# Attention output transposed by DMA, values and w_out cast by GpSimd's DMAs, first keys first

## The chip, the core and the metric

The kernel runs on one core of a Trainium2 chip. The core has TensorE (matmuls, results in PSUM), VectorE, ScalarE and GpSimd (elementwise work), and SyncE (SP), which here only issues transfers. Each engine runs its own stream of instructions in order and waits on semaphores. Sixteen DMA engines move the data; a transfer is issued by SP, ScalarE (the ACT queue) or GpSimd (the POOL queue). The metric is the device time of one execution in microseconds, lower is better.

## The reference

Two layers follow each other. The first is causal attention with 8 batches, 8 heads, 576 positions and a head size of 64; 16 "beacon" keys and values stand ahead of the sequence and are seen by every query. The second is a feed-forward layer on the 4608 x 512 result, with 2048 hidden units and an ELU between its two products.

```python
k_all = np.concatenate([beacon_k, k], axis=2)          # (8, 8, 592, 64)
v_all = np.concatenate([beacon_v, v], axis=2)
scores = scale * np.matmul(q, k_all.transpose(0, 1, 3, 2))
causal[:, Nb:] = np.triu(np.ones((S, S), dtype=bool), k=1)
scores = np.where(causal, -1000000000.0, scores)
a = softmax(scores)
attn = np.matmul(a, v_all)                             # (8, 8, 576, 64)
x = attn.transpose(0, 2, 1, 3).reshape(4608, 512)
h = x @ w_in                                           # 512 x 2048
g = np.where(h > 0.0, h, np.exp(np.minimum(h, 0.0)) - 1.0)
out = g @ w_out                                        # 2048 x 512
```

All inputs and the output are float32 in HBM.

## The kernel before, in words

**Attention.** Two heads are worked on at a time: pair n = 4 b + hp is pair hp of batch b, 32 pairs in all. SP loads its keys and queries in float32 (`load_pair`, L266; the first queries go by the ACT queue). A cast to bf16 (L271, GpSimd or VectorE) is followed by nine transposes on TensorE and one for the beacon keys (L308, L310), and by copies out of PSUM (kT on VectorE, L318 and L319; qT on ScalarE or VectorE, L324 and L326). Then come the scores (L335), their exponentials on ScalarE (L344), the causal mask on GpSimd (L350) and the product with the values (`do_AV`, L369), whose 65th column is the sum of the exponentials. VectorE divides (`do_norm`, L384 and L385) and writes fp16 rows of the attention output into `x16s`. The queries of a batch are cut into five blocks (`BLOCKS`) of 112, 128, 128, 128 and 80 rows.

**Values.** `load_v` (L277, L281) brings a chunk of 128 keys for all heads to a float32 staging tile by SP; `cast_v` (L285) casts it on VectorE into one of two fp16 buffers, which take turns between the batches.

**Turning x.** The feed-forward layer wants x with its 512 features on the partitions. `do_xT` (L395) transposes each block of a pair on TensorE, five transposes per pair, and `do_xcopy` (L402) copies the result from PSUM to `xT` on VectorE. In batch 0 this is done range by range, in the others once per pair.

**Feed-forward.** The tokens are cut into ten tiles (`TILES`): two of 256, eight of 512. For a tile, 16 (or 8) steps of four matmuls or more with w_in (L418) each fill a PSUM buffer. ScalarE takes the exponential (`do_e`, L424), GpSimd clamps it (`do_clamp`, L428), and VectorE joins it with h (`do_join`, L437) into fp16. Then 16 matmuls with w_out per 128 tokens (L445), a copy (L451) and a store by SP (L455). The weights are loaded by SP in pieces of 128 x 512 (`load_w`, L294) and cast by VectorE or GpSimd (`cast_w`, L299). The PSUM buffers of L418, L445, of the values' product and of the x transposes come from the same four ("ff").

**The order.** Nothing of the order is left to a scheduler on the chip. `Plan` is a small list scheduler that runs at build time: every piece of work is an `Op` with an engine, a key, a guessed duration, its dependencies and the buffers that it takes and gives. An engine that is free takes the ready operation with the lowest key; the instructions of each engine are then issued in the order that comes out. Loads go in the order of `FIRST` (i = piece of w_in, o = piece of w_out, k and q = pair, b = beacon keys, v = chunk of values), and after it by keys; SP issues the loads in exactly that order. The constants `SHIFT`, `AT`, `AT0`, `PACES` and `LAG` place batches and tiles in time, `ON_POOL` and `Q_ON_ACT` choose engines. The durations and places are numbers in the code, and what happens on the chip can differ from them.

Of the kernel before, what the change touches and what calls it, by code (L numbers as in the profile page):

```python
# [15 lines left out]
P = 128  # L16
# [96 lines left out]
def kernel(  # L113
# [103 lines left out]
    xT = [big.tile([P, NT], FP16, name=f"xT{cc}") for cc in range(NCC)]  # L217
# [11 lines left out]
    with tc.tile_pool(name="psum", bufs=1, space=bass.MemoryType.PSUM) as psum:  # L229
        slots = {  # L230
# [42 lines left out]

        def load_v(b, jc):
            vst = vsts[b, jc] = stage.tile([P, H, D], FP32, tag="vst", name="vst", bufs=5)
            if jc == 0:
                nc.sync.dma_start(out=vst[0:NB], in_=beacon_v[b].rearrange("h n d -> n h d"))  # L277
            r0 = NB if jc == 0 else 0
            lo = P * jc - NB + r0
            n = kc_sz[jc] - r0  # L280
            nc.sync.dma_start(out=vst[r0:r0 + n], in_=v[b, :, lo:lo + n, :].rearrange("h s d -> s h d"))  # L281
# [13 lines left out]

        def cast_w(which, i):
            fo, cc = divmod(i, NCC)
            dst = w_in16[:, cc, 512 * fo:512 * fo + 512] if which == 0 else w_out16[:, i, :]
            (nc.gpsimd if ON_POOL[which][i] == "1" else nc.vector).tensor_copy(out=dst, in_=wsts[which, i])  # L299

# [152 lines left out]
        def do_store(tt, t4):  # L453
# [5 lines left out]
        SHIFT = [16.14, -0.99, 5.34, 5.22, 2.06, -2.4, 5.6, 10.12]  # L459
        AT = [6.32, -0.92, -1.25, -0.44, -0.32, 1.85, 2.37]  # L460
        AT0 = [[-34.73, -23.83, -34.35, -35.48], [-34.06, -25.35, -36.58, -41.97], [-23.78, -23.81, -5.98, -9.75]]
        PACES = [(-11.97, 2.68, 26.27, 2.47), (-3.71, 3.3, 35.33, 4.82), (35.86, 1.78, 23.69, 3.57), (76.2, 2.29, 30.35, 3.0), (117.45, 1.81, 27.55, 2.07)]
        ON_POOL = ("0100001100101101", "0110011111111010", "00011011")
        LAG = 27.37
        URGE = 44.17
        Q_ON_ACT = "11011010"
        FIRST = (
            "i3 q0 k0 b0 q1 k2 k3 v0 k1 q2 q3 i8 v1 i10 v2 i7 i15 i0 v3 i1 i4 i9 i11 b1 i2 i14 v4 o2 k4 "
            "i6 q4 i13 i5 k5 o4 o8 i12 v5 o7 v6 o6 o1 o5 q5 q6 v8 o0 o12 k6 o13 o9 o15 o3 o10 o14 v9 "
            "o11 v7 k7 q7 ").split()  # L470
# [6 lines left out]
        scaled, last_xT = {}, {}  # L477
# [3 lines left out]
        def load_key(name, key):  # L481
            return FIRST.index(name) - 200 if name in FIRST else key
# [3 lines left out]
        def plan_loads(n):  # L486
            b, hp = divmod(n, HP)
            if hp == 0:
                got = load(load_key(f"b{b}", place(b, 0) - 31), 0.2, partial(load_bk, b), take=["bk"])
                bk_in[b] = add("POOL", place(b, -0.9), 0.6, partial(cast_bk, b),  # L490
                               deps=[got, last_T.get(b - 2)], give=["bk"])
            gots = []
            for is_k in (True, False):
                key = load_key(("k" if is_k else "q") + str(n), place(b, hp) - 30)
                gots.append(load(key, 0.85, partial(load_pair, n, is_k), take=["st"] if is_k else [], issue=0.61))
            on_dve = n < len(ON_POOL[2]) and ON_POOL[2][n] == "0"
            qk_in[n] = add(
                "DVE" if on_dve else "POOL", place(b, hp + AT[0]), 0.9 if on_dve else 1.23,
                partial(cast_pair, n, nc.vector if on_dve else nc.gpsimd), deps=gots + [last_T.get(("pair", n - 2))], take=["sb"], give=["st"])
# [3 lines left out]
        def plan_v(b):  # L503
            for jc in range(NKC):
                key = load_key(f"v{NKC * b + jc}", place(b - 1, 1.8 + 0.4 * jc))
                got = load(key, 1.5, partial(load_v, b, jc), take=["vst"], issue=1.0 if jc == 0 else 0.5)
                v_cast[b, jc] = add(
                    "DVE", place(b, -0.7 + 0.16 * jc), 0.56, partial(cast_v, b, jc),
                    deps=[got, last_AV.get(b - 2)], give=["vst"])

        def plan_w(which, i, key):
            got = load(load_key("io"[which] + str(i), 0), 0.75, partial(load_w, which, i), take=["gt"])
            eng, dur = ("POOL", 0.65) if ON_POOL[which][i] == "1" else ("DVE", 0.55)
            w_at[which, i] = add(eng, key, dur, partial(cast_w, which, i), deps=[got], give=["gt"])

        def plan_pair(n):
# [6 lines left out]
            last_T[b] = last_T["pair", n] = T  # L523
# [27 lines left out]
            for r, groups in enumerate([(0,), (1,), (2,)] if b == 0 else [(0,), (1, 2)]):  # L551
# [7 lines left out]
                last_AV[b] = AV  # L559
                normed.append(add(  # L560
                    "DVE", key - URGE, 0.32 + 0.148 * len(blks), partial(do_norm, n, groups),
                    deps=[AV, last_xT.get(n - 2 * HP)], give=["ff", "av"]))
# [16 lines left out]
        def plan_tile(p):  # L579
# [3 lines left out]
            for b in range(B):  # L583
                for r, (rlo, rhi) in enumerate(CUT.ranges):
                    if b * S + rlo < hi and b * S + rhi > lo:
                        xs += [scaled[b * HP + hp, r] for hp in range(HP)]
# [40 lines left out]
        for i in range(16):  # L627
            plan_w(0, i, place(0, 2.0) + i)
            plan_w(1, i, place(1, 0.5) + i)
# [7 lines left out]
        issues.sort(key=lambda i: i.key)  # L637
        for one, two in zip(issues, issues[1:]):
# [30 lines left out]
```

## Time and profile before

| | us |
|---|---|
| three runs: median | 370.35 |
| lowest | 370.12 |
| the profiled execution | 371.33 |
| its span, first to last instruction | 369.6 |
| TensorE busy | 350.4 (95%) |
| VectorE busy | 235.6 (64%) |
| ScalarE busy | 197.7 (53%) |
| GpSimd busy | 199.0 (54%) |
| first transpose / first scores on TensorE at | 7.9 / 10.9 |
| first L418 matmul / first L445 matmul at | 33.3 / 54.0 |
| last x transpose / last matmul at | 294.9 / 365.7 |

One more run took 1993.31 us and is not used. The page gives the busy time of each engine, the span in 40 slices of 9.24 us, the DMA queues, the chain of work that ended last, and groups of instructions by line with their counts and mean durations. Instructions that only issue a transfer do not count as busy. A matmul's recorded time overlaps with the next one's: four matmuls of 512 columns are 379 ns each by their row, and hold the chain for 0.86 us together. The chain of work says at each moment which instruction the end was waiting for, so the time that a group holds on it is what the group costs.

### The profile page before, as it was taken

How to read it: one execution, taken by the hardware profiler on the slowest of the kernel's cores; microseconds unless marked ns; L12 is line 12 of the kernel's file. 1: busy time of each engine (PE TensorE's matmuls, PEld its weight loads, DVE VectorE, ACT ScalarE, POOL GpSimd, SP SyncE). 2: the span in 40 equal slices, each digit the busy share in tenths (PEclk: the TensorE clock that was granted, in tenths of full speed). 3: DMA queues.
4: the chain of work that ended last, by engine and by line, in shares of the span. 5: the costliest groups of instructions: out<-in, count | busy, mean ns of one | idle time of the engine just before them, and what ended most of it. 6: DMA issues, size and time to landing. Idle time of an engine off the chain costs nothing.

```text
span 369.6 us, 8541 instructions
## 1 busy us (share of the span) xinstructions
PE 350.4 (95%) x3360; PEld 197.8 (54%) x3360; DVE 235.6 (64%) x496; ACT 197.7 (53%) x293; POOL 199.0 (54%) x376
## 2 busy tenths in 40 slices
PE   1688999999999999999999999999999999999995
PEld 1457865645565565555565455555555544444442
DVE  1758898777767668585974756566655555555421
ACT  1566876486658777567646556456563333333200
POOL 4467999576737766566743456454343334333200
PEclk9999999999999999999999999999999999999999
DMA  7999999995493276861455310000000001000022
GB/s 215 290 283 310 309 304 238 292 241 155 124 244 114 66 175 164 215 184 36 125 149 140 102 50 2 30 28 30 31 30 28 31 28 57 31 28 28 30 85 85
DMA packets 58856, 47.21 MB, mean 128 GB/s; under 512 B 41920, under 2 KB 41920, under 8 KB 58816
## 3 DMA queue, kind: packets, MB, share of 16 engines
q1 hardware_dynamic: 58672, 46.38, 44.2%
q8 instruction: 26, 0.43, 0.5%
q10 hardware_dynamic: 144, 0.29, 0.3%
q14 instruction: 14, 0.11, 0.1%
HBM read 37.22 MB, written 9.44 MB: 126 GB/s over the span
## 4 chain that ended last, share of the span: by engine, by line
PE 86%; DVE 4%; POOL 3%; DMA 3%; ACT 1%; issue 1%; SPq 0%; ACTq 0%; POOLq 0%
PE ops L445 34%; PE hps L418 30%; PE av L369 8%; PE sc L335 7%; PE tr L308 4%; DMA st<-in_k_dram 3%; PE xt L395 2%; POOL e L428 1%; DVE gt L437 1%; POOL et L350 1%; DVE kT L318 1%; DVE w_out L299 1%; ACT et L344 1%; ACT qT L324 1%; PE tr L310 0%
## 5 line engine op out<-in xcount | busy, mean ns | idle before, releaser
L418 PE MATMUL hps<-xT,w_in 128*128 128x512 f16 (+1 forms) x640 | 143.7, 358 | 0.5 <-DVE gt L437 0.4
L445 PE MATMUL ops<-w_out,gt 128*128 128x512 f16 x576 | 143.9, 379 | 0.1
L428 POOL TENSOR_SCALAR e<-e 128x512 f32<-128x512 f32 x144 | 89.3, 623 | 97.4 <-ACT e L424 97.4
L437 DVE SCALAR_TENSOR_TENSOR gt<-e,hps 128x512 f16<-128x512 f32 x144 | 97.5, 683 | 63.3 <-POOL e L428 63.1
L424 ACT ACTIVATE e<-hps 128x512 f32<-128x512 f32 x144 | 85.8, 601 | 95.0 <-PE hps L418 93.8
L344 ACT ACTIVATE et<-sc 128x736 f16<-128x736 f32 (+3 forms) x128 | 103.9, 864 | 29.1 <-PE sc L335 25.6
L418 PEld LDWEIGHTS <-w_in 128*128 128x128 f16 x640 | 58.8, 98 | 54.7 <-issue 3.6
L445 PEld LDWEIGHTS <-gt 128*128 128x128 f16 x576 | 52.5, 98 | 57.0 <-issue 2.1
L350 POOL TENSOR_SCALAR_AFFINE_SELECT et<-et 128x256 f16<-128x256 f16 (+2 forms) x160 | 59.9, 400 | 38.3 <-ACT et L344 35.4
L369 PEld LDWEIGHTS <-et 128*128 128x128 f16 (+1 forms) x960 | 37.0, 99 | 9.7 <-issue 1.5
L369 PE MATMUL av<-v,et 128*128 128x65 f16 (+1 forms) x960 | 41.4, 197 | 0.0
L335 PE MATMUL sc<-qT,kT 64*128 64x80 bf16 (+3 forms) x704 | 37.2, 237 | 3.5 <-ACT qT L324 2.0
L451 DVE COPY osb<-ops 128x512 f32<-128x512 f32 x36 | 24.8, 688 | 21.0 <-PE ops L445 20.7
L271 POOL CAST st<-st 128x1152 bf16<-128x1152 f32 x28 | 32.1, 1149 | 7.0 <-POOL et L350 2.2
L335 PEld LDWEIGHTS <-kT 64*128 64x128 bf16 x704 | 21.9, 97 | 22.6 <-issue 14.1
L385 DVE TENSOR_TENSOR x<-av,rl 128x384 f16<-128x384 f32 (+2 forms) x68 | 32.0, 471 | 2.3
L308 PE MATMUL tr<-identb,st 128*128 128x128 bf16 x288 | 23.1, 230 | 9.1 <-DVE st L271 8.5
L318 DVE COPY kT<-tr 128x576 bf16<-128x576 bf16 x32 | 24.1, 753 | 8.1 <-PE tr L310 7.3
L308 PEld LDWEIGHTS <-st 128*128 128x128 bf16 x288 | 19.8, 103 | 14.7 <-DVE st L271 8.9
L384 DVE RECIPROCAL rl<-av 128x6 f32<-128x6 f32 (+2 forms) x68 | 12.5, 183 | 21.5 <-PE av L369 20.9
L324 ACT ACTIVATE qT<-tr 128x576 bf16<-128x576 bf16 x20 | 13.0, 649 | 23.9 <-DVE kT L319 20.7
L285 DVE CAST v<-vst 128x512 f16<-128x512 f32 (+1 forms) x40 | 19.8, 504 | 1.7 <-DMA vst<-in_v_dram 1.7
(26 smaller groups left out, 101.0 us busy)
## 6 DMA issues: line engine op xcount, KB each, us to landing
st<-in_k_dram SPq DMA_DIRECT2D x32, 288.0 KB, 4.4
out_dram<-osb SPq DMA_DIRECT2D x36, 256.0 KB, 2.0
st<-in_q_dram SPq DMA_DIRECT2D x31, 288.0 KB, 4.7
vst<-in_v_dram SPq DMA_DIRECT2D x24, 256.0 KB, 5.4
wst<-in_moe_w_in_dram SPq DMA_DIRECT2D x16, 256.0 KB, 6.5
wst<-in_moe_w_out_dram SPq DMA_DIRECT2D x16, 256.0 KB, 6.0
vst<-in_v_dram SPq DMA_DIRECT2D x8, 224.0 KB, 5.0
vst<-in_v_dram SPq DMA_DIRECT2D x8, 160.0 KB, 5.6
```

What stands on the lines that cost most here:

```text
L271: eng.tensor_copy(out=o.rearrange("p g h d -> p h g d"), in_=f32s[n].rearrange("p h (g d) -> p h g d", g=G))
L308: nc.tensor.transpose(out=tr[:, P * g:P * g + P], in_=b16s[n][:, g].rearrange("p h d -> p (h d)"), identity=identb)
L335: nc.tensor.matmul(out=sc[:, h, o:o + w], lhsT=kT[D * h:D * h + D, P * jc:P * jc + P], rhs=qT[D * h:D * h + D, q0:q0 + w], start=True, sto ...
L344: nc.scalar.activation(out=et[:, :, 0:w], in_=scs[n, u][:, :, 0:w], func=AFT.Exp, bias=0.0, scale=float(1.0 / (D ** 0.5)))
L350: nc.gpsimd.affine_select(out=et[:, :, c0:c0 + dw], in_=et[:, :, c0:c0 + dw], compare_op=ALU.is_ge, fill=fill0, base=q0 + NB - P * jc, pat ...
L369: nc.tensor.matmul(out=av[:, c:c + D + 1], lhsT=ets[n, CUT.unit_of[jc, at]][0:m, h, col:col + P], rhs=v16[0:m, jc, 2 * hp + h, 0:D + 1], s ...
L385: nc.vector.tensor_tensor(out=x16s[b % 2][:, blks[0]:blks[0] + nb, P * hp:P * hp + P].rearrange("q i (h d) -> q i h d", d=D), in0=av[:, :, ...
L418: nc.tensor.matmul(out=hps[:, (hi - lo) * j:(hi - lo) * (j + 1)], lhsT=w_in16[:, cc, P * fc:P * fc + P], rhs=xT[cc][:, lo:hi], start=(cc = ...
L424: nc.scalar.activation(out=e, in_=hpss[tt, i], func=AFT.Exp, bias=0.0, scale=1.0)
L428: nc.gpsimd.tensor_scalar(out=e, in0=e, scalar1=1.0, scalar2=0.0, op0=ALU.min, op1=ALU.max)
L437: nc.vector.scalar_tensor_tensor(out=gt, in0=es[tt, i], scalar=1.0, in1=hpss[tt, i], op0=ALU.subtract, op1=ALU.max)
L445: nc.tensor.matmul(out=ops, lhsT=gts[tt, fc][:, P * t4:P * (t4 + 1)], rhs=w_out16[:, fc, :], start=(fc == 0), stop=(fc == NFC - 1))
```

## The change

Six things are changed together.

1. From batch 1 on (`XB = 1`) x is turned by DMA. The four `xT` tiles become one, and `turn_x` issues on SP one transposing DMA for each block of a batch, with all four pairs at once, after the last pair's division. TensorE's transposes and VectorE's copies stay for batch 0 alone.
2. From batch 2 on (`VB = 2`) the values are loaded by GpSimd's DMAs, which cast to fp16 on the way, straight into the fp16 buffer. The staging tile and VectorE's cast go.
3. All of w_out is loaded by four DMAs of GpSimd, which cast to fp16 on the way; its 16 loads by SP and its 16 casts go. These four wait for nothing.
4. Keys and queries of pair 0 are the first loads on SP and ACT, and w_out is gone from `FIRST`, which has another order.
5. Four pieces of w_in are cast by ScalarE ("2" in `ON_POOL`); fewer by GpSimd.
6. The constants that place the work are other numbers, and a batch's buffers now wait for all its products, not for the last alone.

```diff
-    xT = [big.tile([P, NT], FP16, name=f"xT{cc}") for cc in range(NCC)]
+    xTa = big.tile([P, NCC, NT], FP16, name="xT")
+    xT = [xTa[:, cc] for cc in range(NCC)]
...
+        VB = 2
+        XB = 1
...
+        def turn_x(b, blk):
+            q0, rows, _ = BLOCKS[blk]
+            nc.sync.dma_start_transpose(
+                out=xTa[:, :, b * S + q0:b * S + q0 + rows], in_=x16s[b % 2][0:rows, blk, :])
+
         def load_v(b, jc):
-            vst = vsts[b, jc] = stage.tile([P, H, D], FP32, tag="vst", name="vst", bufs=5)
+            if b >= VB:
+                eng, vst = nc.gpsimd, v16s[b % 2][:, jc, :, 0:D]
+            else:
+                eng = nc.sync
+                vst = vsts[b, jc] = stage.tile([P, H, D], FP32, tag="vst", name="vst", bufs=5)
...
+        def load_wo(f4):
+            nc.gpsimd.dma_start(
+                out=w_out16[:, 4 * f4:4 * f4 + 4, :], in_=moe_w_out[512 * f4:512 * f4 + 512, :].rearrange("(c p) d -> p c d", p=P))
...
+            if ON_POOL[which][i] == "2":
+                nc.scalar.activation(out=dst, in_=wsts[which, i], func=AFT.Copy)
...
-        SHIFT = [16.14, -0.99, 5.34, 5.22, 2.06, -2.4, 5.6, 10.12]
-        AT = [6.32, -0.92, -1.25, -0.44, -0.32, 1.85, 2.37]
+        SHIFT = [10.33, -2.61, 5.48, 3.9, 12.34, 1.61, 18.16, 26.55]
+        AT = [8.06, -1.0, -0.44, -0.82, -0.25, 0.89, 17.62, -15.16, 3.38, -53.58]
...
-        ON_POOL = ("0100001100101101", "0110011111111010", "00011011")
-        LAG = 27.37
+        ON_POOL = ("0200210020102110", "0021220022120010", "10001001")
+        LAG = 23.52
...
-            "i3 q0 k0 b0 q1 k2 k3 v0 k1 q2 q3 i8 v1 i10 v2 i7 i15 i0 v3 i1 i4 i9 i11 b1 i2 i14 v4 o2 k4 "
-            "i6 q4 i13 i5 k5 o4 o8 i12 v5 o7 v6 o6 o1 o5 q5 q6 v8 o0 o12 k6 o13 o9 o15 o3 o10 o14 v9 "
-            "o11 v7 k7 q7 ").split()
+            "b0 k3 q2 k2 i3 k1 q1 v1 q0 i11 k0 i7 q3 i8 i10 i15 v0 i13 i5 v3 i6 v2 i14 i9 i2 q4 b1 i1 "
+            "i12 v4 i0 k4 v5 k5 i4 q5 k6 q6 k7 v8 q7 v6 v9 v7 ").split()
...
-            return FIRST.index(name) - 200 if name in FIRST else key
+            return ["k0", "q0"].index(name) - 900 if name in ("k0", "q0") else FIRST.index(name) - 200 if name in FIRST else key
...
+                if b >= VB:
+                    key = place(b - 1, AT[8] + 0.4 * jc)
+                    got = add("POOL", key, 2.4 if jc == 0 else 1.2, partial(load_v, b, jc), deps=last_AV.get(b - 2, []))
+                    v_cast[b, jc] = add("DMA", key, 1.0, None, deps=[got], lat=2.5)
+                    continue
...
+                if b >= XB:
...
+                    if hp == HP - 1:
+                        for blk in blks:
+                            s = add("SP", at(AT[7]), 1.25, partial(turn_x, b, blk), deps=part.pop(blk))
+                            done = add("DMA", at(AT[7]), 0.5, None, deps=[s], lat=2.2)
...
+                    continue
...
-            plan_w(1, i, place(1, 0.5) + i)
+        for f4 in range(4):
+            got = add("POOL", AT[9] + 3 * f4, 1.5, partial(load_wo, f4))
+            got = add("DMA", -150 + f4, 3.0, None, deps=[got], lat=2.5)
+            w_at.update({(1, 4 * f4 + c): got for c in range(4)})
```

## The prediction

> **What bounds the kernel now.** I read the page's engine totals and slices first, then the table by stage, then the chain of work stage by stage, because a share of the whole span mixes a start that waits with a middle that does not.
>
> ```profile
> PE 350.4 (95%) x3360; PEld 197.8 (54%) x3360; DVE 235.6 (64%) x496; ACT 197.7 (53%) x293; POOL 199.0 (54%) x376
> DMA  7999999995493276861455310000000001000022
> GB/s 215 290 283 310 309 304 238 292 241 155 124 244 114 66 175 164 215 184 36 125 149 140 102 50 2 30 28 30 31 30 28 31 28 57 31 28 28 30 85 85
> ```
>
> TensorE is busy for 95% of the span, and the transfers are full (nine tenths and more) for the first ten slices of 9.24 us. The table by stage separates the two:
>
> ```profile
> core 0: us, PE busy (x) PEld busy (x) DVE busy (x) ACT busy (x) POOL busy (x), PEclk, DMA share, GB/s
> 0.00:10.00 10.00, 1.25 (x10) 0.98 (x10) 2.33 (x10) 1.28 (x1) 3.76 (x19) 1.00 0.77 217
> ...
> 30.00:40.00 10.00, 9.18 (x145) 7.80 (x144) 9.09 (x28) 6.82 (x11) 9.22 (x16) 1.00 1.02 286
> 40.00:60.00 20.00, 19.02 (x225) 13.97 (x224) 18.15 (x35) 15.16 (x25) 19.84 (x35) 1.00 1.03 295
> 60.00:100.00 40.00, 40.00 (x463) 23.22 (x462) 32.03 (x71) 25.49 (x39) 28.33 (x53) 1.00 0.80 215
> ...
> 340.00:370.00 30.00, 25.68 (x119) 11.43 (x117) 8.28 (x13) 2.80 (x5) 3.06 (x5) 1.00 0.17 62
> ```
>
> From 60 us to the last matmul at 365.7 TensorE has no idle time: there only fewer matmuls make the end earlier, and an idle VectorE or GpSimd gains nothing. All that an order of loads can win or lose lies in the first 60 us, where TensorE is idle for 15.3 us, 13.5 of them before 30 us. What follows the last matmul, 3.9 us of copy and store, is not touched.
>
> **Part 1, the transposes.** 140 of the 160 TensorE transposes on L395 go (28 pairs of heads in batches 1 to 7, five each), with 28 VectorE copies on L402. The row of the groups gives 221 ns each, but matmuls overlap, so I price them by the chain, which counts how far each moved the end:
>
> ```profile
> by line: PE hps L418 35.3%; PE ops L445 29.4%; PE av L369 12.3%; PE sc L335 11.7%; PE tr L308 7.5%; PE xt L395 3.5%; PE tr L310 0.8%
> 61 pieces in order of time: start us, us, what
> ...
> 62.00 0.26 PE xt L395 x5
> ```
>
> That is the stage 60 to 100 us. In the six stages of 40 us from 60 to 300 the transposes hold 3.5, 4.4, 3.2, 2.6, 2.6 and 2.6%, together 18.9% of 40 us = 7.6 us, and the table of that tile's instructions counts 25 + 30 + 25 + 20 + 20 + 20 = 140 of them there. Term: **-7.6 us**.
>
> In their place SP issues 35 transposing DMAs (five blocks for each of seven batches), each for all four pairs of a batch. The trace of before has none. By its rows an SP issue takes 0.61 us (a key load) and up to 2.6 where the ring is full, and lands after 2.0 us (a store) to 4.4 us (a key load). The plan writes 1.25 us to issue and 2.7 to land. So the last of five lands some 3 + 2 = 5 to 6.3 + 4.4 = 11 us after the last division. Before, that step took 3.9 us: the last division ended at 291.5 and the last copy of xT at 295.4. Tiles 8 and 9 both need batch 7; they are 2 x 32 groups of four matmuls at 0.864 us = 55.3 us, and from the first matmul of tile 8, at 295.6, there are 70.1 us to the end. So 14.8 us of other matmuls can be done while transposes are under way. At 11 us they cost nothing; I take 0, and price the excess as a rival. SP is also the queue of the loads and stores: a transpose that waits for a division holds them up, but the loads are keyed about 30 us ahead, and 35 x 1.25 = 44 us of SP's time lies in 369.
>
> **Part 2, values by GpSimd.** 30 casts of v (24 x 0.517 + 6 x 0.455) and the 28 copies of 0.452 leave VectorE, 28 us in all, and none of it is on the path after 60 us: 0. What is added are 36 issues on GpSimd, six per batch. The instructions behind such an issue are the clamps (L428), the masks and the casts of keys; VectorE's joins wait for the clamps, and through four PSUM buffers TensorE does. From 60 to 260 us GpSimd is busy for 28.3 + 25.5 + 25.3 + 20.9 + 21.5 = 121.4 of 200 us, so 78.6 us are free: 2.2 us for each of 36. At the 1.2 us of the plan it is 43 us, 82% busy: no cost. SP's own row for such an issue is 0.43 us. I take 0.
>
> **Part 3, w_out by GpSimd.** Sixteen loads leave SP; eleven casts of 0.709 us leave GpSimd, five of 0.836 VectorE. Those casts lie at 32 to 57 us, where TensorE is idle 1.8 us; without them most of that can go: **-1.8**, at most. But where do the four DMAs of 1 MB go? They wait for nothing and have low keys, so the plan puts all four at the head of GpSimd's stream, behind the memsets, which end at 3.8 us. Before, the first w_out load was issued at 22.0 us. So 4.2 MB go beside what the start waits for, while the transfers are full. Two ends. (a) They yield, or what they delay was early anyway: 0. (b) They share by halves: the last w_in piece that the first feed-forward matmul needs (i0, 30th in the list) then has 8.1 MB of SP's loads and 4.2 MB ahead of it; at the rates of the slices (2.0, 2.7, 2.6, 2.9, 2.9 MB per 9.24 us) 12.3 MB are in at 44 us, against 8.1 MB at 30. The first L418 matmul was at 33.3; it would be at 45, nearly 12 us of matmuls are put off, and about 2 us of that was idle or attention anyway: +9.5. The row nearest to the question is who waited for a transfer:
>
> ```profile
> DVE w_in L299 <- DMA wst<-in_moe_w_in_dram: 4.2, 1, 4.2
> POOL bk L258 <- DMA bk<-in_beacon_k_dram: 3.8, 1, 3.8
> ...
> POOL w_in L299 <- DMA wst<-in_moe_w_in_dram: 0.8, 2, 0.7
> ```
>
> The 4.2 us are the very first load; of the other fifteen w_in casts two waited, 0.8 us together, and the chain from 17 to 40 us names TensorE, ScalarE and GpSimd but no transfer. I take **+0.8**, near (a), and keep +9.5 for the range.
>
> [...]
>
> **Part 4, first keys first.** k0 is issued at 0.8 instead of 1.24 us, without 256 KB ahead of it: it could land 1.2 us before the 7.1 of now. But pair 0 is now cast by GpSimd, behind the four issues of part 3: at 1.5 us each these end at 9.8 us, and the first scores come at 14 instead of 10.85. Between -1.2 and +3.5; I take 0, since the next pairs' loads decide (the second group of transposes was at 13.3 already). Four w_in casts of some 0.6 us on ScalarE are hidden: it is idle for about 3 of every 10 us before 40.
>
> **Sum.** 371.33 (the profiled execution: span 369.6 and 1.7 around it) - 7.6 - 1.8 + 0.8 = 362.7. The median of the runs, 370.35, is 1.0 below the profiled time, so I forecast 361.7, say **362**. 2%, 7.4 us, is about what a measurement of this kernel can tell from no change.
>
> **Rivals.**
> 1. *w_out starves the start* (end b): 371.3 - 7.6 + 9.5 - 1.0 = 372. For it: the full transfers of the first ten slices, and 12 MB ahead of i0. Against it: the few waits for w_in.
> 2. *GpSimd becomes the bound*, the one that ends slower: every issue makes 1024 runs of 256 B and is written by the engine that also clamps. It decides from 2.2 us each; at 3 us 36 issues are 108 us where 78.6 are free, +29 us: 391. At 2.5 us it is +11: 373. For it: GpSimd is already 71% busy from 60 to 100 us, with gaps of 0.3 to 1.8 us, shorter than such an issue. Against it: an issue by SP takes 0.43 us.
> 3. *The transposes land late.* The point is 14.8 + 3.9 = 18.7 us after batch 7's last division. At 8.2 us each (the longest landing of a w load), one after the other, five take 41 us: +22 at the end, 384; at 4.4 us each 22 us: +3, 365, and as much again where an earlier tile waits: 368. Against it: transfers on one queue overlap now.
> [...]
> 4. *The start gets better by more*: half of the 13.5 us of idle before 30 us goes: 355. And the change does what it says in no case less than in part 1: the 140 transposes leave TensorE for certain.
>
> **Chances.** Forecast 0.45 (358 to 366; faster than 362.9 for 0.36 of it), start starved 0.22 (366 to 375), GpSimd 0.16 (373 to 395), transposes late 0.12 (364 to 384), better start 0.05 (352 to 358). Faster by over 2% (under 362.9): 0.36 + 0.05 + a little of the others = 0.42. Slower by over 2% (over 377.8): 0.13 of GpSimd, 0.06 of the transposes, 0.02 of the start = 0.21. Within: 0.37. The range 355 to 379 leaves out most of GpSimd, the late half of the transposes, and the best starts: 0.2. The forecast's own range is 358 to 366.
>
> **What would show it.** No xt on L395 after batch 0, and the chain without it. The first L418 matmul at 30 to 35 us (forecast) or near 45 (rival 1). TensorE at 40.00 of 40 from 60 us on; if not, joins waiting for clamps that stand behind GpSimd's issues (rival 2), or L418 matmuls waiting for a transposing DMA (rival 3). The issues' own durations on SP and GpSimd settle the two prices that I had to bound. I am wrong if idle time appears on TensorE after 60 us, or if the start loses more than it gains.

## The result and the profile after

| | us |
|---|---|
| before, median of three runs (370.12 to 371.47) | 370.35 |
| after, median of three runs (379.89 to 382.34) | 381.24 |
| ratio of the runs, 95% interval | 1.0281 (1.0257 to 1.0305): slower |
| forecast, range | 362, 355 to 379 |

One slow run of each kernel is left out, of 1993.31 us before and of 462.42 us after, where TensorE was granted 0.77 of its full clock (with them the medians are 370.91 and 381.79); the latter was the traced one, so what follows is from another execution of the changed kernel, of 379.02 us (span 377.3; before 369.6). The totals of its page:

```profile
PE 343.2 (91%) x3220; PEld 189.5 (50%) x3220; DVE 208.6 (55%) x433; ACT 199.2 (53%) x297; POOL 217.7 (58%) x401
```

TensorE has 140 matmuls fewer and is busy for 7.2 us less. It ends 7.7 us later, so it must have stood idle for 15 us more. The table by stage (length, then busy us and instructions of TensorE, its weight loads, VectorE, ScalarE and GpSimd, the granted clock as a share of full speed, the DMA share, GB/s) says where. First two stages before, then the change:

```profile
10.00:20.00 10.00, 6.81 (x62) 4.93 (x62) 7.06 (x16) 5.68 (x8) 5.25 (x9) 1.00 1.07 280
20.00:30.00 10.00, 8.48 (x118) 5.88 (x114) 5.80 (x21) 7.15 (x9) 5.38 (x13) 1.00 1.07 315
```

```profile
10.00:20.00 10.00, 3.95 (x32) 2.71 (x33) 2.93 (x7) 2.87 (x4) 1.67 (x4) 1.00 1.17 225
20.00:30.00 10.00, 0.82 (x8) 0.55 (x8) 2.90 (x7) 2.56 (x4) 0.61 (x1) 1.00 1.14 283
30.00:40.00 10.00, 8.63 (x101) 5.87 (x98) 8.05 (x25) 5.99 (x9) 5.65 (x13) 1.00 0.98 262
...
80.00:100.00 20.00, 18.06 (x173) 9.32 (x166) 10.60 (x21) 12.17 (x18) 15.00 (x27) 1.00 1.08 157
100.00:140.00 40.00, 40.00 (x456) 22.51 (x453) 24.66 (x53) 27.24 (x41) 30.02 (x54) 1.00 0.90 139
```

| idle time of TensorE, us | before | after | more |
|---|---|---|---|
| 0 to 10 | 8.75 | 8.75 | 0.0 |
| 10 to 20 | 3.19 | 6.05 | 2.9 |
| 20 to 30 | 1.52 | 9.18 | 7.7 |
| 30 to 60 | 1.80 | 4.02 | 2.2 |
| 80 to 100 | 0 | 1.94 | 1.9 |
| 180 to 220 | 0 | 0.12 | 0.1 |

The sum closes: 14.8 us more idle time and 7.2 less busy make 7.6 of the 7.7. Before 60 us 12.8 are lost, between 80 and 100 us 1.9. From 20 to 30 us TensorE does eight matmuls. What it waited for there is in the chain of work up to 62 us, of which these are the summary and the five longest pieces (start, length, what):

```profile
by line: DMA vst<-in_v_dram 23.8%; DMA wst<-in_moe_w_in_dram 22.4%; DMA st<-in_q_dram 10.6%; SPq L306 9.5%; SPq L269 7.4%; PE hps L437 3.1%; DVE v L297 2.9%; ACT et L363 2.9%; SPq L293 2.9%; PE tr L327 2.6%; issue 2.3%; POOL et L369 1.2%; P
...
8.03 4.57 SPq L306
...
14.16 13.91 DMA wst<-in_moe_w_in_dram
...
33.62 6.57 DMA st<-in_q_dram
...
40.21 6.84 DMA vst<-in_v_dram
...
48.05 7.90 DMA vst<-in_v_dram
```

Before, the chain between 17 and 40 us named no transfer; now a piece of w_in that took 13.9 us to land, and then batch 1's first queries and two chunks of its values, hold the end. The two longest waits of TensorE in that stage tell how (start, length, what; in brackets the idle time before it and what ended that):

```profile
22.46 0.43 DVE L297 CAST v<-vst 128x512 f16<-128x512 f32 x1 [5.80 <-DMA vst<-in_v_dram]
23.89 0.43 DVE L318 CAST w_in<-wst 128x512 f16<-128x512 f32 x1 [1.00 <-DMA wst<-in_moe_w_in_dram]
24.23 0.75 DVE L337 COPY kT<-tr 128x576 bf16<-128x576 bf16 x1
25.85 0.51 PE L354 MATMUL sc<-qT,kT 64*128 64x256 bf16 x4 [7.35 <-ACT qT L343]
...
28.09 0.63 ACT L316 ACTIVATE w_in<-wst 128x512 f16<-128x512 f32 x1 [2.29 <-DMA wst<-in_moe_w_in_dram]
...
29.68 1.12 PE L327 MATMUL tr<-identb,st 128*128 128x128 bf16 x9 [3.33 <-ACT et L363]
```

The keys for the 7.35 us wait had been transposed at 17.9 us. Their copy stood in VectorE's stream behind two casts of late loads, a chunk of values and a piece of w_in, that TensorE did not need yet. In the same way ScalarE's exponentials stood behind a cast of w_in. The w_out transfers beside them, by the instructions on that tile:

```profile
L309 POOL DMA_DIRECT2D w_out<-in_moe_w_out_dram x4: 755/766/919, 3.7 to 6.1; - x4
...
DMA to landing us min/median/max: 11.3/15.3/21.1
```

They were issued between 3.7 and 6.9 us, and the last landed at 27.2. The first feed-forward matmul comes late, and so does the first with w_out, though w_out was there long before:

```profile
L437 PE MATMUL hps<-xT,w_in x640: 269/379/390, 45.8 to 352.2; 128*128 128x512 f16 x128, 128*128 128x256 f16 x32
L464 PE MATMUL ops<-w_out,gt x576: 377/379/390, 64.7 to 372.9; 128*128 128x512 f16 x192
```

45.8 and 64.7 us, against 33.3 and 54.0 before.

### The profile page after: what moved, and what is told of

It is laid out like the page before. It is cut to its first block, busy times and chain, and to the rows that moved or that the text cites. A ratio compares the mean times of both kernels' runs of the same rounds, so it can differ in the third digit from the quotient of the medians.

```text
span 460.7 us, 8311 instructions
## 1 busy us (share of the span) xinstructions
PE 431.1 (94%) x3220; PEld 216.0 (47%) x3220; DVE 210.8 (46%) x433; ACT 200.8 (44%) x297; POOL 218.6 (47%) x401
## 4 chain that ended last, share of the span: by engine, by line
PE 90%; DMA 5%; SPq 3%; DVE 1%; ACT 0%; issue 0%
PE ops L464 36%; PE hps L437 34%; PE av L388 8%; PE sc L354 7%; PE tr L327 4%; DMA wst<-in_moe_w_in_dram 3%; DMA vst<-in_v_dram 2%; SPq L306 1%; SPq L269 1%; SPq L293 0%; PE tr L329 0%; PE xt L414 0%; ACT et L363 0%; DVE v L297 0%; DVE x L404 0%
## 5 line engine op out<-in xcount | busy, mean ns | idle before, releaser
L464 PE MATMUL ops<-w_out,gt 128*128 128x512 f16 x576 | 183.2, 459 | 0.0
L437 PE MATMUL hps<-xT,w_in 128*128 128x512 f16 (+1 forms) x640 | 182.8, 431 | 0.2 <-DVE x L404 0.2
L363 ACT ACTIVATE et<-sc 128x768 f16<-128x768 f32 (+3 forms) x128 | 103.7, 862 | 40.1 <-PE sc L354 38.6
L437 PEld LDWEIGHTS <-w_in 128*128 128x128 f16 x640 | 67.7, 111 | 79.9 <-issue 74.2
L464 PEld LDWEIGHTS <-gt 128*128 128x128 f16 x576 | 60.2, 110 | 84.5 <-issue 81.7
L388 PEld LDWEIGHTS <-et 128*128 128x128 f16 (+1 forms) x960 | 43.2, 106 | 14.5 <-issue 12.9
L388 PE MATMUL av<-v,et 128*128 128x65 f16 (+1 forms) x960 | 47.3, 208 | 0.8 <-DVE v L297 0.8
L404 DVE TENSOR_TENSOR x<-av,rl 128x256 f16<-128x256 f32 (+2 forms) x68 | 32.1, 471 | 2.3
L403 DVE RECIPROCAL rl<-av 128x4 f32<-128x4 f32 (+2 forms) x68 | 12.6, 185 | 44.2 <-PE av L388 43.7
L293 POOL DMA_DIRECT2D v<-in_v_dram x30 | 26.2, 873 | 0.9 <-issue 0.9
## 6 DMA issues: line engine op xcount, KB each, us to landing
w_out<-in_moe_w_out_dram POOLq DMA_DIRECT2D x4, 512.0 KB, 15.3
```

The source lines that it names most:

```text
L363: nc.scalar.activation(out=et[:, :, 0:w], in_=scs[n, u][:, :, 0:w], func=AFT.Exp, bias=0.0, scale=float(1.0 / (D ** 0.5)))
L388: nc.tensor.matmul(out=av[:, c:c + D + 1], lhsT=ets[n, CUT.unit_of[jc, at]][0:m, h, col:col + P], rhs=v16[0:m, jc, 2 * hp + h, 0:D + 1], s ...
L404: nc.vector.tensor_tensor(out=x16s[b % 2][:, blks[0]:blks[0] + nb, P * hp:P * hp + P].rearrange("q i (h d) -> q i h d", d=D), in0=av[:, :, ...
L437: nc.tensor.matmul(out=hps[:, (hi - lo) * j:(hi - lo) * (j + 1)], lhsT=w_in16[:, cc, P * fc:P * fc + P], rhs=xT[cc][:, lo:hi], start=(cc = ...
L464: nc.tensor.matmul(out=ops, lhsT=gts[tt, fc][:, P * t4:P * (t4 + 1)], rhs=w_out16[:, fc, :], start=(fc == 0), stop=(fc == NFC - 1))
```

## The experiments

The theories at the start: **1**, w_out's DMAs (and batch 2's values) go ahead of what the start waits for; **2**, GpSimd's issues delay the work behind them; **3**, the transposing DMAs land late. Six of the kernels below (e7 to e11 and e13) are built on the changed code with all constants, the order of loads and the engines of the kernel before, which is meant to give the order of instructions of before; each then takes one part of the change, and its edit is shown against that base. No run measured the base by itself; the nearest sign is e9, where TensorE is idle for 15.0 us before 60 us, against 15.3 before. The places of the added instructions (`AT[7]` for the transposes, `AT[8]` for the values, -53.58 for w_out) are those of the change, and no other places were tried in these kernels.

### The change again

> The changed kernel itself once more, since the trace at hand was taken at a granted clock of 0.77. If the start is what costs (theory 1: w_out's four DMAs and then batch 2's values go ahead of what the start waits for), the first L437 matmul stands near 45 us and the first L464 near 64, against 33.3 and 54.0 before, and TensorE has no idle time after some 65 us. If GpSimd's issues (theory 2) or late transposing DMAs (theory 3) cost, TensorE has idle time between 65 and 345 us, in L437 behind joins or behind DMAs.

379.02 us in one run; it is the trace read above. First L437 at 45.8 and L464 at 64.7, TensorE full but for 1.9 us between 80 and 100 and 0.1 us later. That is theory 1, with a small share of theory 3.

The trace also shows how it happens. Two windows of 5 us, by DMA queue (packets, MB, share of 16 engines; q0 is GpSimd's, q1 is SP's), and last SP's queue in the second window before the change:

```profile
q0 software_dynamic: 523, 0.52, 62.7%
q1 hardware_dynamic: 494, 0.75, 49.4%
...
q0 software_dynamic: 776, 0.77, 90.6%
q1 hardware_dynamic: 779, 0.22, 30.7%
...
q1 hardware_dynamic: 2027, 1.25, 105.1%
```

The first pair is 10 to 15 us, the second 15 to 20. In each window the two queues moved about as many packets, 523 and 494, 776 and 779, and not as many bytes. The MB are those written: 0.77 MB in 776 packets are 1 KB each, cast from 2 KB of float32, and such a packet took 93 ns of an engine (0.906 x 16 x 5 us / 776). In the second window SP's queue was at a chunk of values, in packets of 256 bytes: 0.22 MB got through in 5 us, about a sixth of the 1.25 MB that this queue moved in the same window before the change. At 779 packets in 5 us a chunk of values, 1024 packets, needs 6.6 us beside w_out, and at the 2027 of before, larger ones among them, 2.5 (estimates from these counts). The first chunk of values was issued at 6.2 us and landed 16.3 us later; before the change it took 6.3.

How a DMA engine chooses between two queues no view shows; the counts are all that is measured.

### w_out issued later

```diff
-            got = add("POOL", AT[9] + 3 * f4, 1.5, partial(load_wo, f4))
+            got = add("POOL", AT[9] + 3 * f4, 1.5, partial(load_wo, f4), deps=[w_at[0, 0]])
```

> w_out's four DMAs are issued by GpSimd only after the last masks of batch 0, just ahead of the first clamps (they depend on the cast of i0 in the plan); all else as in the change. Theory 1 (w_out in front starves the start): the first L437 matmul goes back from 45 to 32 to 36 us, and the time from 381.8 to 366 to 372. Theory 2 (GpSimd's issues of values) and theory 3 (transposes land late): the time stays within 3 us of 381.8.

391.6 us, ratio 1.058 (1.0544 to 1.0616), outside both expectations. The first L437 went back to 32.8 us as theory 1 has it, and the time went the wrong way by 10 us. The stages 40 to 60 us show why:

```profile
40.00:50.00 10.00, 4.96 (x38) 3.52 (x38) 3.64 (x7) 4.25 (x7) 5.30 (x10) 0.83 1.21 206
50.00:60.00 10.00, 5.87 (x67) 3.97 (x67) 4.17 (x9) 3.40 (x5) 1.94 (x4) 0.66 1.14 258
```

The same starvation, 20 us later: GpSimd's queue now moves 773 packets while SP's, at batch 1's values, moves 774 (45 to 50 us), and a chunk of values holds the chain for 17.85 us from 36.6 on. The first L464 was at 64.7 as in the change; w_out itself had landed by 53.4. So theory 1 was right on what starves, and wrong that the place is the cause: at either place, in the windows counted here, SP's queue moved about as many packets as GpSimd's, whatever it needed at that time.

### x back on TensorE

```diff
-        XB = 1
+        XB = 8
-        AT = [8.06, -1.0, -0.44, -0.82, -0.25, 0.89, 17.62, -15.16, 3.38, -53.58]
+        AT = [8.06, -1.0, -0.44, -0.82, -0.25, 0.89, 2.37, -15.16, 3.38, -53.58]
```

> x is turned on TensorE in all batches as before the change (the place of those transposes, AT[6], is that of the kernel before, 2.37); all else as in the change. If the 35 transposing DMAs work as the prediction's part 1 has it, TensorE gets 7.6 us of matmuls back and the time is 381.8 + 7.6 = 389. Theory 3 (transposes land late and stall TensorE): the time falls below 379.

385.59 us, 1.0401 (1.0383 to 1.0419). Inside the change the transposing DMAs are worth some 3 to 7 us (385.6 against 379.0 to 382.3). The 389 of part 1 was not reached, and theory 3 asked for less than 379: TensorE has 7.3 us more to do, and of the 2.1 us that it stood idle after 60 us 1.1 are left. Late transposes are not what makes the change, as it stands, slower.

### Values back on SP

```diff
-        VB = 2
+        VB = 8
```

> The values of all batches go by SP and VectorE's casts as before (VB = 8), so GpSimd issues only w_out's four DMAs; all else as in the change. Theory 2 (36 issues on GpSimd delay the clamps): the time falls to 372 or less. Theory 1: w_out alone starves the start, and the time stays within 3 us of 381.8; if batch 2's values in front of batch 1's share in it, some 3 to 6 us come back, all before 65 us.

377.56 us, 1.019 (1.0165 to 1.0215): 1.5 to 4.8 us faster than the runs of the change. Idle time between 50 and 60 us falls from 1.28 to 0.39 us and the 1.94 us between 80 and 100 are gone; 0.71 come up at 60 to 80 and 0.98 at 100 to 140. Theory 2 asked for 372 or less, so GpSimd's values are not the main cost inside the change. They have a share in it, and not only before 65 us as expected. What is left, with the first L437 at 45.6 us, is the start.

### w_out by GpSimd, alone in the kernel before

```diff
-            plan_w(1, i, place(1, 0.5) + i)
+        for f4 in range(4):
+            got = add("POOL", -53.58 + 3 * f4, 1.5, partial(load_wo, f4))
...
```

> The kernel before with one part of the change: all of w_out by GpSimd's four casting DMAs at the head of its stream (its 16 loads by SP and its 16 casts go). Theory 1, as the last runs have sharpened it (GpSimd's ring and SP's ring take turns packet by packet, so each 2 KB packet of w_out costs a load of SP one packet's turn, whenever the four are issued): the first L418 matmul (L427 here) moves from 33.3 to 42 to 47 us, and the time is 10 to 16 us longer, 381 to 387. If w_out only hurts together with the change's own order of loads, it stays within 4 us of 371.

380.55 us, 1.0287 (1.0247 to 1.0326): this part alone costs what the whole change costs. It is what theory 1 has, by half a us below both of its ranges: the first feed-forward matmul is at 41.4 us, and a chunk of values holds the chain for 16 us.

```profile
9.76 16.00 DMA vst<-in_v_dram
...
L422 PE MATMUL hps<-xT,w_in x640: 269/379/390, 41.4 to 354.1; 128*128 128x512 f16 x128, 128*128 128x256 f16 x32
```

### w_out back on SP

```diff
-        for f4 in range(4):
-            got = add("POOL", AT[9] + 3 * f4, 1.5, partial(load_wo, f4))
...
+            plan_w(1, i, place(1, 0.5) + i)
-            "i12 v4 i0 k4 v5 k5 i4 q5 k6 q6 k7 v8 q7 v6 v9 v7 ").split()
+            "i12 v4 i0 k4 v5 k5 i4 o1 o2 q5 o3 o0 k6 q6 o4 o5 k7 v8 o6 q7 o7 v6 o8 o9 v9 o10 v7 o11 o12 o13 o14 o15 ").split()
```

> The change with w_out back on SP: 16 loads of 128 x 512 behind i0 in the list of first loads, interleaved with batch 1's, and 16 casts by VectorE, GpSimd and ScalarE. Theory 1: the first feed-forward matmul is back at 32 to 35 us, no load is behind w_out, and the time falls from about 380 to 365 to 370. If the issues of values or the transposes cost as much, it stays above 374.

382.62 us, 1.0327 (1.0286 to 1.0368). A miss by 13 us, and the most telling one. The start is mended (first L437 at 34.1, first L464 at 54.0 us), and the time is no better: idle time came back later, 3.2 us at 40 to 60, 0.9 at 60 to 80, 3.2 at 80 to 100 and 4.1 at 100 to 140. In the chain of work from 40 to 150 us (110 us) the transposing DMAs now hold 10.9%:

```profile
by line: PE hps L437 26.5%; PE ops L464 16.3%; DMA xT<-x 10.9%; PE av L388 7.8%; POOL e L447 6.8%; DMA wst<-in_moe_w_out_dram 6.8%; PE sc L354 5.6%; PE tr L327 3.7%; issue 3.2%; SPq L279 2.3%; POOL et L369 2.3%; POOL v L293 1.9%; SPq L306 1
```

So a start that is on time brings to light what the late start had covered: the transposing DMAs with 12 us of the chain, and GpSimd's issues of values with 2. But w_out's own load holds it for 7.4 us as well (from 53.3 on), at a place in the list that this experiment chose; with w_out earlier in the list the time could be shorter, which was not tried.

### w_out and values back on SP

```diff
-        VB = 2
+        VB = 8
```

> As e5_wo_by_sp, and the values of all batches by SP and VectorE's casts too (VB = 8): GpSimd issues no DMA at all, and of the change are left the transposing DMAs, the order of loads and the constants. If batch 2's values share the rings with batch 1's loads as w_out does, this is 2 to 4 us faster than e5_wo_by_sp, 362 to 367. If GpSimd's issues cost nothing by themselves, it is within 1 us of it or slower (30 casts are back on VectorE).

377.32 us, 1.0167 (1.0118 to 1.0216), 5.3 us faster than the last, where 2 to 4 were expected. So values by GpSimd cost some 5 us once the start is on time. What is left is 12 us above the 365 in the middle of the expectation.

### The transposing DMAs, alone in the kernel before

```diff
-        XB = 8
+        XB = 1
```

> The kernel before, its constants and its order of loads, with one part of the change: x turned by the 35 transposing DMAs from batch 1 on. If the prediction's part 1 holds (140 transposes leave TensorE, and the DMAs land while other matmuls run): 371 - 7.6 = 363.4, 362 to 365. If matmuls wait for transposing DMAs, as two L437 matmuls did for 5 us between 80 and 100 us in the change's own trace, it is 365 to 370, with that idle time on TensorE between 60 and 120 us.

381.38 us, 1.0272 (1.023 to 1.0315), far outside both expectations. TensorE's stages:

```profile
60.00:70.00 10.00, 9.03 (x125) 5.52 (x124) 8.38 (x20) 4.49 (x6) 6.42 (x12) 1.00 1.02 275
70.00:80.00 10.00, 5.75 (x82) 3.25 (x78) 3.36 (x8) 5.04 (x6) 4.96 (x10) 1.00 1.17 219
80.00:90.00 10.00, 6.76 (x39) 2.84 (x40) 2.40 (x4) 3.22 (x5) 2.67 (x6) 0.66 0.84 202
```

These stages were full before. SP's queue and the waiting matmuls tell the story of batch 1:

```profile
69.84 4.08 SPq L279 DMA_TRANSPOSE xT<-x  x2
74.01 0.55 SPq L474 DMA_DIRECT2D out_dram<-osb  x1
74.61 0.42 SPq L293 DMA_DIRECT2D vst<-in_v_dram  x1
75.13 1.61 SPq L269 DMA_DIRECT2D st<-in_k_dram  x1
76.80 0.60 SPq L269 DMA_DIRECT2D st<-in_q_dram  x1
77.49 0.55 SPq L293 DMA_DIRECT2D vst<-in_v_dram  x1
78.13 4.11 SPq L279 DMA_TRANSPOSE xT<-x  x3
...
83.24 4.51 PE L437 MATMUL hps<-xT,w_in 128*128 128x512 f16 x12 [6.51 <-DMA xT<-x]
```

The last division before the three issues ended at 72.0 us (VectorE's L404 at 71.47 for 0.56). By then SP was with the first two blocks, 2 us each where such an issue takes 1.25 in the median; then come a store and four loads, which the plan had put there, and the last three are issued only from 78.1 on. The second of these took 3.8 us to land, and the matmul that needs it had waited for 6.5 us. From the division to the matmul are 11.2 us, the upper end of my 5 to 11; but the matmuls that TensorE could do in between were used up after 4.7. And the twelve matmuls behind the wait take 4.51 us; twelve with no wait before them took 2.75 in this same trace (at 101.0 us). The clock column says 0.66. How much of the six us on SP comes from `AT[7]`, a place that was chosen for the change's order and not for this one, no run tells.

From 60 to 220 us TensorE has 13.7 us of idle time that it did not have before (and 0.5 less before 60). It is busy for 347.5 us, 2.9 less than before where the change, with the same matmuls, has 7.2 less: slow matmuls take the other 4.3. 13.7 - 0.5 - 2.9 = 10.3, against 10.1 us between the two spans.

### The same on ScalarE's queue

```diff
-            nc.sync.dma_start_transpose(
+            nc.scalar.dma_start_transpose(
-                            s = add("SP", at(AT[7]), 1.25, partial(turn_x, b, blk), deps=part.pop(blk))
+                            s = add("ACT", at(AT[7]), 1.25, partial(turn_x, b, blk), deps=part.pop(blk))
```

> As e7_before_turn_dma, with all 35 transposing DMAs issued by ScalarE on its own queue instead of SP (in the plan they take 1.25 us of ScalarE). Theory 3a (the transposes are late because they stand in SP's queue behind loads whose issue waits for a full ring or a free buffer): the five of batch 1 land within some 8 us of the last division, the idle time of 12 us between 60 and 140 us goes for the most part, and the time is 363 to 370. Theory 3b (the transposing transfers themselves are slow beside full traffic): they land as late as on SP and the time stays at 378 or more, ScalarE's lost time added.

394.26 us, 1.0623 (1.059 to 1.0656). Worse by 13 us, and it tells 3a and 3b only in part. Batch 1's last block landed at 79.9 instead of 83.5 us, 8.0 us after the last division as 3a has it, so SP's queue had cost 3.6 us there. But each issue now takes 1.2 to 2.3 us from ScalarE, whose exponentials everything waits for (the chain from 50 to 140 us has 9.6% on these issues), and the 35 transfers land no faster: 4.0 us in the median and 7.2 at most, against 2.6 and 7.3 on SP. Both the place in SP's queue and the transfer itself make them late; what each is worth in the whole kernel this run does not part.

### Transposing DMAs from batch 4 on

```diff
-        XB = 8
+        XB = 4
```

> As e7_before_turn_dma, with the DMAs only from batch 4 on (XB = 4), when the transfers are no longer full: 16 pairs, so TensorE gets 16 x 0.27 = 4.3 us. If only the full traffic before 100 us makes the transposes late, the time is 366 to 368; if they are late in every batch, by a stall of 1 to 2 us each as e7 shows between 140 and 220 us, it is 369 to 374.

366.05 us, 0.9865 (0.9848 to 0.9881): **faster than both kernels**, though by less than the 2% that the prediction takes as telling. It gains 4.9 us where 16 pairs x 0.27 = 4.3 were expected, and TensorE is busy for 4.2 us less. By its table by stage TensorE is full from 60 to 340 us, and the transposes land undisturbed:

```profile
L279 SPq DMA_TRANSPOSE xT<-x x20: 1192/1254/1906, 158.7 to 288.6; - x20
DMA to landing us min/median/max: 2.3/2.5/4.2
```

So the price per pair of the prediction is right, and the saving is real in the later batches, where the DMAs are not full (share 0.61 at 140 to 180 us, 0.50 at 180 to 220 and 0.13 to 0.17 up to 300 in this trace, against 1.09 at 60 to 80).

### Values by GpSimd, alone in the kernel before

```diff
-        VB = 8
+        VB = 2
```

> The kernel before with one part of the change: values of batches 2 to 7 by GpSimd's casting DMAs. At the measured 0.87 us per issue 36 issues take 31 us of GpSimd, where 78.6 are free, so theory 2 in the form of the prediction (GpSimd saturates from 2.2 us) gives 369 to 372. If the 128-byte packets of these DMAs take turns with the loads on SP's ring as w_out's do, batch 1's and 2's loads come late and it is 373 to 378, with idle time on TensorE before 100 us.

387.44 us, 1.0447 (1.0423 to 1.047), far above both expectations. It is theory 2 after all, at a place that the prediction did not look at:

```profile
40.00:60.00 20.00, 16.19 (x183) 12.20 (x180) 16.69 (x32) 12.14 (x20) 19.33 (x35) 1.00 1.05 289
60.00:80.00 20.00, 13.39 (x148) 8.92 (x149) 6.13 (x16) 6.13 (x8) 11.16 (x17) 0.74 0.78 157
```

From 40 to 60 us GpSimd was busy for 19.84 of 20 us already before the change, with w_out's casts and the clamps. Batch 2's six issues (0.87 us each for a chunk, 0.57 for the beacons) fall at 38 to 40 and 59 to 63 us, where it had no time for them. TensorE waited first for joins, and then for a cast of keys that stood behind three issues:

```profile
60.45 2.49 POOL L293 DMA_DIRECT2D v<-in_v_dram  x3
62.92 2.25 POOL L274 CAST st<-st 128x1152 bf16<-128x1152 f32 x2
...
64.15 1.14 PE L327 MATMUL tr<-identb,st 128*128 128x128 bf16 x9 [3.31 <-POOL st L274]
```

TensorE is idle for 6.6 us in 60 to 80 us and runs at 0.74 of its clock there. SP's ten loads of values landed in 6.6 us in the median, the same ten before in 6.2, so the other branch of the expectation, late loads, is not what shows. How much of the 6.6 us each wait caused is not taken apart. Nor is it the whole: the traced span is 17.2 us longer than before, of which 12.2 are idle time (2.8 at 40 to 60 us, 2.3 at 80 to 100) and 5.0 slower matmuls. In the change itself this part costs less; w_out's casts are gone from GpSimd there (14.9 busy us of 20 at 40 to 60), which is a likely reason that no run tests alone.

### First keys first

```diff
-            "i3 q0 k0 b0 q1 k2 k3 v0 k1 q2 q3 i8 v1 i10 v2 i7 i15 i0 v3 i1 i4 i9 i11 b1 i2 i14 v4 o2 k4 "
+            "q0 k0 b0 i3 q1 k2 k3 v0 k1 q2 q3 i8 v1 i10 v2 i7 i15 i0 v3 i1 i4 i9 i11 b1 i2 i14 v4 o2 k4 "
```

> As e9_turn_from_4, with the first piece of w_in moved behind k0, q0 and b0 in the list of first loads: part 4 of the prediction alone. k0 has 256 KB less ahead of it, so the first transposes come 0.5 to 1.3 us earlier. If the loads of the next pairs decide, as the prediction took it, the time stays within 0.7 us of e9_turn_from_4's 366.0; if the first pair decides, it falls by 1 us or more, to 365 or less.

366.59 us, 0.9892 (0.9872 to 0.9911), within 0.7 us of e9_turn_from_4 as expected. The first transposes start at 6.0 instead of 7.6 us, and nothing is gained: 0.3 us less idle time before 10 us, 0.7 more from 10 to 20.

### The change with its three costs undone

```diff
-        XB = 1
+        XB = 4
-        AT = [8.06, -1.0, -0.44, -0.82, -0.25, 0.89, 17.62, -15.16, 3.38, -53.58]
+        AT = [8.06, -1.0, -0.44, -0.82, -0.25, 0.89, 2.37, -15.16, 3.38, -53.58]
```

(on e6_wo_v_by_sp)

> The change with its three costs undone together: w_out and all values by SP, and transposing DMAs only from batch 4 on (AT[6] as before, 2.37); what is left of it are the DMAs of batches 4 to 7, the order of loads, the casts on ScalarE and the constants. If w_out in front, values by GpSimd and early transposes are all that makes the change slow, it is within 2 us of e9_turn_from_4, 364 to 368. If the change's order and constants cost something of their own, it is 370 or more.

371.22 us, 1.0012 (0.9993 to 1.003), 6.1 us faster than e6_wo_v_by_sp and 5 slower than e9_turn_from_4. There is a fourth cost in the order and constants of this kernel. Most of it lies in the start: TensorE is idle for 4.4 us from 10 to 20 and 3.0 from 20 to 30 (2.9 and 1.8 in e9_turn_from_4); before 60 us that makes 2.9 us more, and from 100 to 180 us there are another 1.2, together the 4.1 by which the two traced spans differ. The places of w_out in this list are the experiment's and not the change's, and a load of w_out holds the chain for 5.7 us from 34.4 on, so a part of the 5 us can be theirs; that stays open.

### Transposing DMAs from batch 3 on

```diff
-        XB = 8
+        XB = 3
```

> As e9_turn_from_4, with batch 3 turned by DMA as well: 4 more pairs, so TensorE gets 1.1 us more. If transposes stall only beside full traffic (before 100 us), it is 364.5 to 365.5. If the stalls between 140 and 220 us that e7_before_turn_dma shows come from batch 3, it is 366 to 368.

367.78 us, 0.9913 (0.9884 to 0.9942), as expected if batch 3 brings stalls: it costs more than it gives. TensorE is idle for 0.3 us at 140 to 180 and 1.4 at 180 to 220, more than the 1.1 that four pairs save.

## Why the prediction was wrong

The step that failed is part 3, the +0.8 us for w_out's four DMAs: the start lost 12.8 us. Two more terms that were put at nothing, the landing of the transposes and the issues of values, failed as well, but in the change they cost less (a stall of 1.9 us, and 1.5 to 4.8 us).

- **What bounds the kernel**: right. TensorE's busy and idle time add up to the result within 0.1 us, and all of the loss but 2 us lies before 60 us. One row was misread: the transfers are at nine tenths in slices 2 to 9, not in the first ten (the digits are 7, eight times 9, then 5); nothing in the sum hangs on it.
- **Part 1, -7.6 for the transposes**: right in size. TensorE is busy for 7.2 us less in the change, and e9_turn_from_4 gained 4.9 for 16 pairs where the same price gives 4.3. The issue took 1.25 us, 6.3 for the five of a batch, and the landing 2.4 to 6.7 us; in e9_turn_from_4 a block landed 2.5 us after its issue in the median. The full ring beside the 2.6 us is the author's word for what the rows of before show: an issue of 2.63 us for a piece of w_in at 11.73 us, behind two chunks of values of 1024 packets each, issued at 9.70 and 10.80 us. **The cover was wrong**: the prediction read the 14.8 us of other matmuls at batch 7 and used it for all batches. At batch 1 of e7_before_turn_dma it was 4.7 us. In the change the stall was only 1.9 us: there SP issued the last three blocks 0.9 us after the division, not 6.1, and the matmul came 7.3 us after it, not 11.2. Alone the late landings cost 18 us (10.8 + 7.6).
- **Part 2, values at no cost**: 0.88 us per issue, below the plan's 1.2 and far below the 2.2 from which GpSimd would saturate. But that limit was taken from the mean of 200 us, and the issues of batch 2 fall into 20 us in which GpSimd had 0.16 us free. In the change they cost 1.5 to 4.8 us, alone 16.
- **Part 3, +0.8 for w_out in front**: this is the step that failed. The prediction had both ends and chose (a) by the row of waits: only two of fifteen w_in casts had waited for a transfer. That row tells that the loads came in time with one queue. It says nothing on how early they came, nor on what stands behind such a cast on its engine, nor on what is left when a second queue moves as many packets (776 to 779 in e0_after). End (b) placed the first feed-forward matmul at 45 us, and it came at 45.8. That is partly luck: (b) shared bytes by halves, and what came out about equal in the trace were packets, so that SP's queue got 0.75 MB in one window of 5 us and 0.22 in the next. Its price of 9.5 us was too low too: it took off 2 us for idle time and attention, but attention stood still as well (eight matmuls from 20 to 30 us), because casts of late loads stood ahead of its copies and exponentials, and SP's queue stayed behind after w_out had landed (batch 1's values landed at 45.6 to 58.1 us, before at 37.6 to 55.1). The start lost 12.8 us; w_out's DMAs alone, in e4_before_wo_pool, cost 10.0. The nearer row was in the trace of before: q0 on ACT's queue and i3 on SP's, both issued at 0.8 us, landed side by side, after 5.4 and 4.6 us. The -1.8 us for the casts never came: 30 to 60 us has 2.2 us more idle time, not less.
- **Part 4, 0**: right. The first scores were at 11.0 us against 10.85, and e11 shows that an earlier first pair is worth nothing.
- **Rivals**: rival 1 is what happened, at 0.22, and its 372 was some 9 us short. With the measured terms, 371.3 - 7.2 + 14.8 = 378.9, the sum gives the traced execution; why three other runs took 379.9 to 382.3 is not shown. Rivals 2 and 3 were each real, hidden behind it. The prediction treated them as alternatives; they are three costs that partly cover each other: each alone 10 to 16 us in the kernel before, at the change's places, all together 10 to 11.

## What to carry to other kernels

A transfer moved to another issuer was not out of the way here: w_out's queue moved 776 packets in 5 us while SP's moved 779, and a chunk of values, in packets of 256 bytes, landed after 16.3 us instead of 6.3. So price such a transfer by packets against the loads that the critical stage needs, for the time when it runs, not for when it is needed. A load that is late without being needed yet still holds all the work that stands behind its cast on an engine (a wait of 7.35 us on TensorE here). A limit taken from a mean over the kernel, of an engine's free time or of other work to do, hides the stage that decides; take it from the stage in which the added instructions fall. And when several parts of a change each look free, try them one at a time: a stall at the start can hide two more behind it, while the one good part (here the transposes of the late batches, 1.3% faster than before) drowns.

## What was not expected of the hardware

After an idle time of 6.5 us (e7_before_turn_dma) TensorE did the next twelve matmuls of 512 columns in 4.51 us, where twelve without a wait took 2.75. After one of 1.94 us, in the change itself, twelve took 2.76 (second line; the first is e7's row without a wait):

```profile
101.01 2.75 PE L437 MATMUL hps<-xT,w_in 128*128 128x512 f16 x12
...
87.07 2.76 PE L437 MATMUL hps<-xT,w_in 128*128 128x512 f16 x12 [1.94 <-DMA xT<-x]
```

So the long stall cost 1.8 us more than its length, and the short one nothing more. The granted clock was 0.66 at 80 to 90 us in e7_before_turn_dma and 1.00 at 80 to 100 us in the change. Why the one cost more than itself and the other not, no run tells.
